# A decode step over a 1 GB KV cache: one load queue with shared 4 MB buffers, long VectorE instructions, and V streamed instead of loaded as weights

## The chip, the cores and the metric

The kernel runs on one core of one Trainium2 chip. The metric is the device time of one execution in microseconds (us). Times are medians of several runs; the profile is one more execution, taken by the hardware profiler.

In the profile PE is TensorE (matmuls), PEld its weight loads, DVE VectorE, ACT ScalarE, POOL GpSimd, SP SyncE. A core has 16 DMA engines, which carry all loads. A load "lands" when its last byte has arrived; since its parts run on all 16 engines, it has a first and a last landing, and what I call the spread is the time between the two.

## The reference

It is one token's attention over a long cache, mixed with a small feed-forward block (FFN):

```python
q = (x @ wq)                                   # x: 1x1x512, wq: 512x4096 -> 32 heads of 128
scores = einsum("bhqd,bhkd->bhqk", q, k_cache) * 128**-0.5   # k_cache: 1x32x65536x128 bf16
p = softmax(scores)
o = einsum("bhqk,bhkd->bhqd", p, v_cache)      # v_cache: 1x32x65536x128 bf16
a = o @ wo                                     # wo: 4096x512
b = (silu(x @ w_gate) * (x @ w_up)) @ w_down   # 512x1792, 512x1792, 1792x512
g = sigmoid((x * gate_w).sum())
return g * a + (1 - g) * b
```

K and V are 537 MB each. Every byte is used once, so the kernel has to stream 1087.6 MB (the profile's "HBM read") through the core. All else is small, except that each K row needs a 128-long dot product with q, which VectorE computes.

## The kernel before

A "tile" below is 16,384 rows of one head: 4 MB of K and 4 MB of V. There are 128 of them. K comes in 4 MB pieces on SyncE's queue (32 KB contiguous per partition), V in 2 MB pieces on ScalarE's queue (16 KB per partition). The dot products are computed in chunks of 32 columns (4096 rows): one multiplication into a separate buffer `prod`, four halving additions, and one reduction of the last eight.

```python
for ci, c in enumerate(seg_chunks):            # 4 chunks a tile
    m = c % DMA_MULT                           # DMA_MULT = 4
    if m == 0:
        K_big = kpool.tile([P, DMA_MULT * J, Dh], bf16)      # 2 buffers of 32 KB a partition
        nc.sync.dma_start(out=K_big, in_=A_k_cache[0, h, c*W:(c+DMA_MULT)*W, :]
                          .rearrange("(p j) d -> p j d", j=DMA_MULT * J))
    K_t = K_big[:, m * J : (m + 1) * J, :]     # J = 32
    prod = prodpool.tile([P, J, Dh], bf16)
    nc.vector.tensor_tensor(out=prod, in0=K_t, in1=q_rep, op=ALU.mult)
    half = Dh
    while half > 8:
        half //= 2
        nc.vector.tensor_tensor(out=prod[:, :, 0:half], in0=prod[:, :, 0:half],
                                in1=prod[:, :, half : 2 * half], op=ALU.add)
    nc.vector.tensor_reduce(out=S_sb[:, ci*J:(ci+1)*J], in_=prod[:, :, 0:8], axis=AXIS.X, op=ALU.add)
nc.scalar.activation(out=P_sb, in_=S_sb, func=ACT.Exp, scale=scale, accum_out=rowsum[...])
for ci, c in enumerate(seg_chunks):
    ...                                        # V_big: 2 MB on nc.scalar's queue, 3 buffers, VDMA_MULT = 2
    for j in range(J):                         # V is the weight, one column of P moves
        nc.tensor.matmul(O_ps[:, h:h+1], lhsT=V_t[:, j, :], rhs=P_sb[:, col:col+1],
                         start=(gcol == 0), stop=(gcol == NB - 1))
if h == FFN_POS:                               # FFN_POS = 0: after head 0
    _compute_ffn()
    _load_wo()
... # after all heads: totals of all heads, one normalisation, 32 projections, the mix
```

The softmax here doesn't subtract the row's maximum and nothing guards it: scores larger than these inputs give would overflow.

Of the kernel before, what the change touches and what calls it, by code (L numbers as in the profile page):

```python
# [8 lines left out]
ALU = mybir.AluOpType  # L9
AXIS = mybir.AxisListType  # L10
P = 128

KT_BUFS = 2
VT_BUFS = 3
PROD_BUFS = 2
WMAX = 4096
CHUNKS_PER_SEG = 4
LAST_HEAD_SPLIT = 1
DMA_MULT = 4
VDMA_MULT = 2  # L20
WO_ENG = "sync"
WQ_ENG = "sync"
FFN_ENG = "scalar"
FFN_POS = 0
WQ_FIRST = 0
# [3 lines left out]
def kernel(  # L29
# [24 lines left out]
    W = min(WMAX, Sk)  # L54
    assert Sk % W == 0
    NCH = Sk // W
    J = W // P
    NB = Sk // P
    CPS = min(CHUNKS_PER_SEG, NCH)
    assert NCH % CPS == 0  # L60
    SEGCOLS = CPS * J
    assert SEGCOLS <= 512
    assert NCH % DMA_MULT == 0 and NCH % VDMA_MULT == 0
    HG = 4 if H % 4 == 0 else H
    scale = float(Dh) ** -0.5

    engs = {"gpsimd": nc.gpsimd, "sync": nc.sync, "scalar": nc.scalar}

    consts = ctx.enter_context(tc.tile_pool(name="consts", bufs=1))
    psum_o = ctx.enter_context(tc.tile_pool(name="psum_o", bufs=1, space=bass.MemoryType.PSUM))  # L70
    psum_misc = ctx.enter_context(tc.tile_pool(name="psum_misc", bufs=2, space=bass.MemoryType.PSUM))
# [3 lines left out]
    xT = consts.tile([P, KT], bf16, name="xT")  # L75
    nc.sync.dma_start(out=xT, in_=A_x[0, 0, :].rearrange("(t p) -> p t", p=P))  # L76
    x_row = consts.tile([1, D], bf16, name="x_row")
    nc.sync.dma_start(out=x_row, in_=A_x[0])
    gw_row = consts.tile([1, D], bf16, name="gw_row")
    nc.sync.dma_start(out=gw_row, in_=gate_w.unsqueeze(0))  # L80
    q_bc_sb = consts.tile([P, H * Dh], bf16, name="q_bc_sb")
    b_sb = consts.tile([1, D], f32, name="b_sb")
    gval = consts.tile([1, 1], f32, name="gval")
    oT = consts.tile([P, H], bf16, name="oT")

    X_bc = consts.tile([P, KT, P], bf16, name="X_bc")
    for t in range(KT):
        nc.vector.tensor_copy(out=X_bc[:, t, :], in_=xT[:, t : t + 1].to_broadcast([P, P]))  # L88

    wq_pool_outer = None  # L90
    wq_sb = None
    awq = A_wq.rearrange("(t p) f -> p t f", p=P)
    if WQ_FIRST:
        wq_pool_outer = tc.tile_pool(name="wq_pool", bufs=1)
        wq_pool_o = wq_pool_outer.__enter__()
        wq_sb = wq_pool_o.tile([P, KT, H * Dh], bf16, name="wq_sb")
        engs[WQ_ENG].dma_start(out=wq_sb, in_=awq)

    kpool = ctx.enter_context(tc.tile_pool(name="kt", bufs=KT_BUFS))
    vpool = ctx.enter_context(tc.tile_pool(name="vt", bufs=VT_BUFS))  # L100
    prodpool = ctx.enter_context(tc.tile_pool(name="prod", bufs=PROD_BUFS))
    spool = ctx.enter_context(tc.tile_pool(name="s_sb", bufs=3))
    ppool = ctx.enter_context(tc.tile_pool(name="p_sb", bufs=3))

    def _compute_q(wq_tile):
        for g in range(H // HG):
            qg_ps = psum_misc.tile([P, HG * Dh], f32, name="qg_ps", tag="misc")
            for t in range(KT):
                nc.tensor.matmul(  # L109
                    qg_ps,  # L110
                    lhsT=X_bc[:, t, :],
                    rhs=wq_tile[:, t, g * HG * Dh : (g + 1) * HG * Dh],
                    start=(t == 0),
                    stop=(t == KT - 1),
                )
            nc.scalar.activation(  # L116
                out=q_bc_sb[:, g * HG * Dh : (g + 1) * HG * Dh], in_=qg_ps, func=ACT.Copy
            )

    if WQ_FIRST:  # L120
        _compute_q(wq_sb)
        wq_pool_outer.__exit__(None, None, None)
    else:
        with tc.tile_pool(name="wq_pool", bufs=1) as wq_pool:
            wq_sb = wq_pool.tile([P, KT, H * Dh], bf16, name="wq_sb")
            engs[WQ_ENG].dma_start(out=wq_sb, in_=awq)
            _compute_q(wq_sb)

    awg = B_w_gate.rearrange("(t p) f -> p t f", p=P)
    awu = B_w_up.rearrange("(t p) f -> p t f", p=P)  # L130
    awd = B_w_down.rearrange("(t p) n -> p t n", p=P)

    def _compute_ffn():
        with tc.tile_pool(name="ffn_w", bufs=1) as wpool:
            gu_ps = psum_misc.tile([P, 2 * FT], f32, name="gu_ps", tag="misc")
            wg_sb = wpool.tile([P, KT, F], bf16, name="wg_sb")
            engs[FFN_ENG].dma_start(out=wg_sb, in_=awg)
            wu_sb = wpool.tile([P, KT, F], bf16, name="wu_sb")
            (nc.sync if FFN_ENG == "scalar" else engs[FFN_ENG]).dma_start(
                out=wu_sb, in_=awu  # L140
            )
            wd_sb = wpool.tile([P, FT, D], bf16, name="wd_sb")
            engs[FFN_ENG].dma_start(out=wd_sb, in_=awd)
            for ft in range(FT):
                for wi, wsb in enumerate((wg_sb, wu_sb)):
                    for t in range(KT):
                        nc.tensor.matmul(  # L147
                            gu_ps[:, wi * FT + ft : wi * FT + ft + 1],
                            lhsT=wsb[:, t, ft * P : (ft + 1) * P],
                            rhs=xT[:, t : t + 1],  # L150
                            start=(t == 0),
                            stop=(t == KT - 1),
                        )
            gu_sb = consts.tile([P, 2 * FT], f32, name="gu_sb")
            nc.vector.tensor_copy(out=gu_sb, in_=gu_ps)
            eg = consts.tile([P, FT], f32, name="eg")
            nc.scalar.activation(out=eg, in_=gu_sb[:, :FT], func=ACT.Exp, scale=-1.0)
            nc.vector.tensor_scalar_add(eg, eg, 1.0)
            nc.vector.reciprocal(eg, eg)
            hprod = consts.tile([P, FT], f32, name="hprod")  # L160
            nc.vector.tensor_tensor(out=hprod, in0=gu_sb[:, :FT], in1=eg, op=ALU.mult)
            hT = consts.tile([P, FT], bf16, name="hT")
            nc.vector.tensor_tensor(out=hT, in0=hprod, in1=gu_sb[:, FT:], op=ALU.mult)
            b_ps = psum_misc.tile([1, D], f32, name="b_ps", tag="misc")
            for ft in range(FT):
                nc.tensor.matmul(  # L166
                    b_ps,
                    lhsT=hT[:, ft : ft + 1],
                    rhs=wd_sb[:, ft, :],
                    start=(ft == 0),  # L170
                    stop=(ft == FT - 1),
                )
            nc.vector.tensor_copy(out=b_sb, in_=b_ps)  # L173

            xg = consts.tile([1, D], f32, name="xg")
            s_t = consts.tile([1, 1], f32, name="s_t")
            nc.vector.tensor_tensor_reduce(
                out=xg, in0=x_row, in1=gw_row, scale=1.0, scalar=0.0,
                op0=ALU.mult, op1=ALU.add, accum_out=s_t,
            )  # L180
            eg2 = consts.tile([1, 1], f32, name="eg2")
            nc.scalar.activation(out=eg2, in_=s_t, func=ACT.Exp, scale=-1.0)  # L182
            nc.vector.tensor_scalar_add(eg2, eg2, 1.0)  # L183
            nc.vector.reciprocal(gval, eg2)

    wo_holder = {}

    def _load_wo():
        wo_pool = ctx.enter_context(tc.tile_pool(name="wo_pool", bufs=1))
        wo_sb = wo_pool.tile([P, H, D], bf16, name="wo_sb")  # L190
        engs[WO_ENG].dma_start(out=wo_sb, in_=A_wo.rearrange("(h p) n -> p h n", p=P))
        wo_holder["wo"] = wo_sb

    if FFN_POS < 0:
        _compute_ffn()
        _load_wo()

    seg_plans = []
    for h in range(H):
        if h == H - 1 and LAST_HEAD_SPLIT and CPS > 1:  # L200
            chunks = list(range(NCH))
            plan = [chunks[i : i + CPS] for i in range(0, max(NCH - CPS, 0), CPS)]
            remaining = chunks[len(plan) * CPS :]
            for cc in remaining:
                plan.append([cc])
        else:
            plan = [list(range(i, i + CPS)) for i in range(0, NCH, CPS)]
        seg_plans.append(plan)
    NSEGMAX = max(len(pl) for pl in seg_plans)

    psum_a = ctx.enter_context(tc.tile_pool(name="psum_a", bufs=1, space=bass.MemoryType.PSUM))
    psum_tot = ctx.enter_context(tc.tile_pool(name="psum_tot", bufs=1, space=bass.MemoryType.PSUM))
# [5 lines left out]
    for h in range(H):  # L218
# [60 lines left out]
        if h == FFN_POS:  # L279
            _compute_ffn()  # L280
            _load_wo()
# [65 lines left out]
```

## Time and profile before

| what | before | where it is read |
|---|---|---|
| time, median of 5 runs | 2584.27 us (2582.68 to 2587.85) | timed runs |
| span of the profiled execution | 2582.6 us | first line of the page |
| DMA engines, share taken by the two load queues | 49.7% + 49.4% | queue table |
| VectorE busy | 2470.5 us, 96% | busy table |
| TensorE busy, granted clock | 502.3 us, 19%; 0.51 | busy table; per-core list |
| last input byte to end of span | 18.4 us | DMA records and span |

These are lines of the profile page of the kernel before. First the busy table; then the span in 40 equal slices, one character or number each (busy tenths for VectorE, granted TensorE clock in tenths, busy tenths of the DMA engines, GB/s moved); then the DMA queues with packets, MB and share of the 16 engines' time; then the chain of work that ended last.

```profile
span 2582.6 us, 37723 instructions
...
PE 502.3 (19%) x16576; PEld 468.9 (18%) x16576; DVE 2470.5 (96%) x3093; ACT 58.6 (2%) x273; POOL 0.4 (0%) x5
...
DVE  4969999999999999999999999999999999999995
...
PEclk8555555555555555555555555555555555555555
DMA  9999999999999999999999999999999999999996
GB/s 404 421 399 426 427 428 431 430 429 426 428 429 428 427 430 422 429 426 428 428 427 428 427 424 431 425 428 425 429 429 422 430 426 428 425 427 430 424 427 276
DMA packets 63498, 1090.06 MB, mean 422 GB/s; under 512 B 6755, under 2 KB 12646, under 8 KB 13670
...
q1 hardware_dynamic: 24134, 547.11, 49.7%
q10 hardware_dynamic: 39200, 540.56, 49.4%
q8 instruction: 129, 2.11, 0.3%
q14 instruction: 35, 0.29, 0.0%
...
DMA 75%; DVE 18%; PE 6%; issue 0%; SPq 0%; ACT 0%; DVEq 0%; ACTq 0%
```

Both DMA and VectorE look full, and one has to decide which of the two paces. After the first four slices, which hold a dip to 399, all but the last move 422 to 431 GB/s. The queue table also shows a third kind of traffic, q8 and q14: the program's own instructions are fetched by the same engines, 2.4 MB of them for 37,723 instructions.

The next lines are groups of instructions of the kernel before, with shapes kept apart: line, engine, operation, output and input with their shapes, count, busy time, mean ns of one, and the idle time before them with what ended it.

```profile
L241 DVE TENSOR_TENSOR prod<-K_big,q_bc_sb 128x4096 bf16<-128x4096 bf16 x512 | 1147.0, 2278 | 52.4 <-DMA K_big<-in_A_k_cache_dram 51.5
L245 DVE TENSOR_TENSOR prod<-prod 128x2048 bf16<-128x2048 bf16 x512 | 600.9, 1212 | 0.0
...
L249 DVE TENSOR_REDUCE S_sb<-prod 128x32 f32<-128x256 bf16 x512 | 187.2, 403 | 0.5 <-DVE prod L245 0.5
```

Busy time over count gives 1147.0/512 = 2240 ns for a multiplication of 4096 elements per partition, less than the mean of 2278 because instructions of two chunks alternate and overlap a little. Fitting busy time over count of the five TENSOR_TENSOR sizes (4096 elements down to 256) gives 0.52 ns per element plus 107 ns per instruction; with the mean durations it is 145 ns, so about 38 ns of each instruction are hidden by the overlap.

The last views are three windows (busy time of each engine with the number of instructions, granted clock, DMA share, GB/s) and the end of the timeline (start, duration, engine, line, operation, tiles, count, idle time before and what ended it).

```profile
160.00:180.00 20.00, 1.25 (x47) 1.20 (x45) 1.34 (x1) 0.00 (x0) 0.00 (x0) 0.50 1.05 434
180.00:200.00 20.00, 1.49 (x56) 1.49 (x56) 20.00 (x25) 0.40 (x2) 0.00 (x0) 0.50 0.89 367
300.00:320.00 20.00, 3.55 (x128) 3.57 (x128) 20.00 (x26) 0.40 (x2) 0.00 (x0) 0.50 1.00 427
```

```profile
2564.67 1.87 PE L272 MATMUL O_ps<-P_sb,V_big 128*128 128x1 bf16 x64 [3.00 <-DMA V_big<-in_A_v_cache_dram]
...
2569.01 9.95 PE L301 MATMUL a_ps<-wo_sb,oT 128*1 128x512 bf16 x32 [1.51 <-DVE oT L297]
...
2578.99 0.68 DVE L310 TENSOR_TENSOR diff<-a_ps,b_sb 1x512 f32<-1x512 f32 x1 [10.04 <-PE a_ps L301]
```

The windows show where the two limits met badly. VectorE starts late (38.9 us into the span, by the timeline) and stands nearly still from 160 to 180 us, waiting for K: wo had been issued ahead of that K load, and its 1 KB rows ran from 137 to 163 us by the packet records. VectorE is then full for the next 20 us, in which DMA moves only 367 GB/s. The tail shows 32 projection matmuls taking 9.95 us after everything else.

One thing lies in the code of the kernel before and not in its profile. K is laid out with 128 consecutive rows on each partition and V with 64, so the probability in one column belongs to another row than the V row that it multiplies. I found this by reading the access patterns; no run tests it (before_v32k, below, happens to load both in one layout). These inputs hide it: the scores are near zero, the probabilities almost equal. The changed kernel uses one layout for both, so it does not have this mismatch.

### The profile page before, as it was taken

Reading aid. Unit: us, or ns where it says so; the run is one execution under the profiler, and the core shown is the slowest. Engines: PE = TensorE matmul, PEld = TensorE weight load, DVE = VectorE, ACT = ScalarE, POOL = GpSimd, SP = SyncE. Lnnn points to the kernel's source line nnn. Section 1 sums busy time; section 2 is a strip of 40 time slices with the busy share of each in tenths; the row PEclk is TensorE's granted clock in tenths of the full one; section 3 lists DMA queues with packets and bytes.
Section 4 is the critical chain, followed back from the end, with each engine's and each line's share of the span. In section 5 each row is a group of like instructions: output and inputs, shape, how many; then the busy total and the mean of one; then the engine's idle time right before and its main releaser. Section 6 shows DMA issues by size and latency. Waiting matters only on the chain.

```text
span 2582.6 us, 37723 instructions
## 1 busy us (share of the span) xinstructions
PE 502.3 (19%) x16576; PEld 468.9 (18%) x16576; DVE 2470.5 (96%) x3093; ACT 58.6 (2%) x273; POOL 0.4 (0%) x5
## 2 busy tenths in 40 slices
PE   2211112112121121112121112211121221112124
PEld 1211112111111111111111111111111111111112
DVE  4969999999999999999999999999999999999995
ACT  1000000000000000000000000000000000000000
POOL 0000000000000000000000000000000000000000
PEclk8555555555555555555555555555555555555555
DMA  9999999999999999999999999999999999999996
GB/s 404 421 399 426 427 428 431 430 429 426 428 429 428 427 430 422 429 426 428 428 427 428 427 424 431 425 428 425 429 429 422 430 426 428 425 427 430 424 427 276
DMA packets 63498, 1090.06 MB, mean 422 GB/s; under 512 B 6755, under 2 KB 12646, under 8 KB 13670
## 3 DMA queue, kind: packets, MB, share of 16 engines
q1 hardware_dynamic: 24134, 547.11, 49.7%
q10 hardware_dynamic: 39200, 540.56, 49.4%
q8 instruction: 129, 2.11, 0.3%
q14 instruction: 35, 0.29, 0.0%
HBM read 1087.64 MB, written 0.00 MB: 421 GB/s over the span
## 4 chain that ended last, share of the span: by engine, by line
DMA 75%; DVE 18%; PE 6%; issue 0%; SPq 0%; ACT 0%; DVEq 0%; ACTq 0%
DMA V_big<-in_A_v_cache_dram 72%; DVE prod L245 9%; DVE prod L241 9%; PE O_ps L272 5%; DMA K_big<-in_A_k_cache_dram 3%; DVE S_sb L249 1%; PE a_ps L301 0%; PE b_ps L166 0%; PE tot_ps L284 0%; DVE out_sb L312 0%; DVE diff L310 0%; ACT P_sb L254 0%; DVE b_sb L173 0%; SPq L76 0%; DVE tot_sb L286 0%
## 5 line engine op out<-in xcount | busy, mean ns | idle before, releaser
L241 DVE TENSOR_TENSOR prod<-K_big,q_bc_sb 128x4096 bf16<-128x4096 bf16 x512 | 1147.0, 2278 | 52.4 <-DMA K_big<-in_A_k_cache_dram 51.5
L245 DVE TENSOR_TENSOR prod<-prod 128x2048 bf16<-128x2048 bf16 (+3 forms) x2048 | 1184.3, 645 | 0.0
L272 PE MATMUL O_ps<-P_sb,V_big 128*128 128x1 bf16 x16384 | 474.7, 166 | 2025.8 <-DMA V_big<-in_A_v_cache_dram 1632.3
L272 PEld LDWEIGHTS <-V_big 128*128 128x128 bf16 x16384 | 457.4, 104 | 2043.5 <-DMA V_big<-in_A_v_cache_dram 1777.3
L249 DVE TENSOR_REDUCE S_sb<-prod 128x32 f32<-128x256 bf16 x512 | 187.2, 403 | 0.5 <-DVE prod L245 0.5
L254 ACT ACTIVATE P_sb<-S_sb 128x128 bf16<-128x128 f32 (+1 forms) x131 | 40.2, 307 | 2470.4 <-PE O_ps L272 1469.3
L254 ACT ACTIVATION_READ_ACCUMULATOR P_sb<-S_sb 128x1 f32 x131 | 24.4, 186 | 0.0
L88 DVE COPY X_bc<-xT 128x128 bf16<-128x128 bf16 x4 | 0.6, 222 | 14.5 <-DMA xT<-in_A_x_dram 14.5
L183 DVE TENSOR_SCALAR eg<-eg 1x1 f32<-1x1 f32 x1 | 0.1, 142 | 14.8 <-ACT eg L182 14.8
L109 PE MATMUL qg_ps<-wq_sb,X_bc 128*128 128x512 bf16 x32 | 8.4, 429 | 29.2 <-DMA wq_sb<-in_A_wq_dram 29.2
L286 DVE COPY tot_sb<-tot_ps 128x224 f32<-128x224 f32 x1 | 0.4, 390 | 13.4 <-PE tot_ps L284 13.4
L310 DVE TENSOR_TENSOR diff<-a_ps,b_sb 1x512 f32<-1x512 f32 x1 | 0.7, 678 | 10.0 <-PE a_ps L301 10.0
L301 PE MATMUL a_ps<-wo_sb,oT 128*1 128x512 bf16 x32 | 9.9, 486 | 1.5 <-DVE oT L297 1.5
L109 PEld LDWEIGHTS <-X_bc 128*128 128x128 bf16 x32 | 3.4, 107 | 33.7 <-DVE X_bc L88 15.9
L147 PE MATMUL gu_ps<-xT,wg_sb 128*128 128x1 bf16 x56 | 3.0, 165 | 19.3 <-DMA wg_sb<-in_B_w_gate_dram 19.3
L147 PEld LDWEIGHTS <-wg_sb 128*128 128x128 bf16 x56 | 2.6, 104 | 19.8 <-issue 19.8
L116 ACT ACTIVATE q_bc_sb<-qg_ps 128x512 bf16<-128x512 f32 x8 | 4.8, 597 | 29.8 <-PE qg_ps L109 29.8
L166 PE MATMUL b_ps<-wd_sb,hT 128*1 128x512 bf16 x14 | 5.2, 549 | 0.0
L301 PEld LDWEIGHTS <-oT 128*1 128x1 bf16 x32 | 3.1, 101 | 8.4 <-issue 4.2
L147 PE MATMUL gu_ps<-xT,wu_sb 128*128 128x1 bf16 x56 | 3.2, 166 | 0.8 <-DMA wu_sb<-in_B_w_up_dram 0.8
L147 PEld LDWEIGHTS <-wu_sb 128*128 128x128 bf16 x56 | 2.7, 104 | 0.9 <-DMA wu_sb<-in_B_w_up_dram 0.9
L173 DVE COPY b_sb<-b_ps 1x512 f32<-1x512 f32 x1 | 0.7, 678 | 1.8 <-PE b_ps L166 1.8
(24 smaller groups left out, 9.0 us busy)
## 6 DMA issues: line engine op xcount, KB each, us to landing
V_big<-in_A_v_cache_dram ACTq DMA_DIRECT2D x256, 2048.0 KB, 26.1
K_big<-in_A_k_cache_dram SPq DMA_DIRECT2D x128, 4096.0 KB, 19.8
wq_sb<-in_A_wq_dram SPq DMA_DIRECT2D x1, 4096.0 KB, 27.2
wo_sb<-in_A_wo_dram SPq DMA_DIRECT2D x1, 4096.0 KB
wu_sb<-in_B_w_up_dram SPq DMA_DIRECT2D x1, 1792.0 KB
wg_sb<-in_B_w_gate_dram ACTq DMA_DIRECT2D x1, 1792.0 KB, 19.1
wd_sb<-in_B_w_down_dram ACTq DMA_DIRECT2D x1, 1792.0 KB
xT<-in_A_x_dram SPq DMA_DIRECT2D x1, 1.0 KB, 14.9
```

Source lines behind the costliest of these rows:

```text
L109: nc.tensor.matmul(qg_ps, lhsT=X_bc[:, t, :], rhs=wq_tile[:, t, g * HG * Dh : (g + 1) * HG * Dh], start=(t == 0), stop=(t == KT - 1),)
L116: nc.scalar.activation(out=q_bc_sb[:, g * HG * Dh : (g + 1) * HG * Dh], in_=qg_ps, func=ACT.Copy)
L147: nc.tensor.matmul(gu_ps[:, wi * FT + ft : wi * FT + ft + 1], lhsT=wsb[:, t, ft * P : (ft + 1) * P], rhs=xT[:, t : t + 1], start=(t == 0), ...
L166: nc.tensor.matmul(b_ps, lhsT=hT[:, ft : ft + 1], rhs=wd_sb[:, ft, :], start=(ft == 0), stop=(ft == FT - 1),)
L173: nc.vector.tensor_copy(out=b_sb, in_=b_ps)
L241: nc.vector.tensor_tensor(out=prod, in0=K_t, in1=q_rep, op=ALU.mult)
L245: nc.vector.tensor_tensor(out=prod[:, :, 0:half], in0=prod[:, :, 0:half], in1=prod[:, :, half : 2 * half], op=ALU.add,)
L249: nc.vector.tensor_reduce(out=S_sb[:, ci * J : (ci + 1) * J], in_=prod[:, :, 0:8], axis=AXIS.X, op=ALU.add,)
L254: nc.scalar.activation(out=P_sb[:, :segcols], in_=S_sb[:, :segcols], func=ACT.Exp, scale=scale, accum_out=rowsum[:, h * NSEGMAX + sgi : h ...
L272: nc.tensor.matmul(O_ps[:, h : h + 1], lhsT=V_t[:, j, :], rhs=P_sb[:, col : col + 1], start=(gcol == 0), stop=(gcol == NB - 1),)
L301: nc.tensor.matmul(a_ps, lhsT=oT[:, h : h + 1], rhs=wo_sb[:, h, :], start=(h == 0), stop=(h == H - 1),)
L310: nc.vector.tensor_tensor(out=diff, in0=a_ps, in1=b_sb, op=ALU.subtract)
```

## The change

The intent: free memory by computing the dot products inside K's own buffer, use it for five equal buffers that K, V and all weights share, put all loads in order on one queue in 4 MB pieces, make VectorE's instructions four times as long, let TensorE stream V past four columns of P instead of loading V as weights, start on the first K piece earlier, and move all of the tail's work that can be done early ahead of the last V tile. The core of the diff, shortened:

```diff
-KT_BUFS = 2; VT_BUFS = 3; PROD_BUFS = 2; WMAX = 4096; DMA_MULT = 4; VDMA_MULT = 2
+KPP = 128; SLOTS = 5; VB = 4; DEFER = 1
+slots = ctx.enter_context(tc.tile_pool(name="slots", bufs=SLOTS))     # 32 KB a partition each
 # loads
-nc.sync.dma_start(out=K_big, ...)          # 4 MB
-nc.scalar.dma_start(out=V_big, ...)        # 2 MB
+nc.sync.dma_start(out=t[:, at:at+m, :], in_=src[:, at:at+m, :])   # K and V, m = 128: 4 MB
+load("k", 0, [KPP // 4] * 4)               # first K tile in four pieces, after 1 MB of wq
 # scores
-prod = prodpool.tile([P, J, Dh], bf16)     # J = 32
-nc.vector.tensor_tensor(out=prod, in0=K_t, in1=q_rep, op=ALU.mult)
+w = K_t[:, i*J:(i+1)*J, :]                 # parts = 1: J = 128
+nc.vector.tensor_tensor(out=w, in0=w, in1=q_rep, op=ALU.mult)
 # P times V
-for j in range(J):
-    nc.tensor.matmul(O_ps[:, h:h+1], lhsT=V_t[:, j, :], rhs=P_sb[:, col:col+1], ...)
+for i in range(KPP // VB):                 # O_ps is 4 x 512 now
+    nc.tensor.matmul(O_ps[h], lhsT=P_sb[:, i*VB:(i+1)*VB],
+                     rhs=V_t[:, i*VB:(i+1)*VB, :].rearrange("p a b -> p (a b)"), ...)
+# once per head: copy O_ps to SBUF, pick its four diagonal 128-blocks and add them (4 fp32 matmuls),
+# normalise it (deferred behind the next head's second tile)
-if h == FFN_POS: _compute_ffn(); _load_wo()
+if n == N - 2: load_tail_weights()          # wo, gate, up, down ahead of the last V tile
+load("v", N - 1, [64, 32, 16, 16])          # the last V tile in four pieces
+if n == N - 1: ffn(); 31 projections        # ahead of the last tile's P times V
```

## The prediction

> **What bounds the kernel now.** The DMA queue table shows the 16 DMA engines at 99% of their time (49.7% + 49.4% for two queues); the slices show 427 to 428 GB/s almost throughout. VectorE is busy 96%, and the windows from 300 to 500 us show both at 100%. The grouped instructions give VectorE's need per 128x16384 K tile: four chunks of 4.83 us, 19.3 us. DMA needs 8.39 MB / 428 GB/s = 19.6 us for that tile and its V. So DMA is the bound by a hair. The chain of waits agrees: 75% DMA, 18% VectorE. The last bytes land at about 2561.5 us; the remaining 21 us are PV, totals, 32 projections (10 us), output.
>
> **What changes.**
> - VectorE: the same elements in 128-column instead of 32-column instructions. By form, one costs 0.52 ns per element plus 107 ns (the reduce 1.04 ns plus 99). New tile: 8.64+4.37+2.24+1.17+0.64+1.17 = 18.2 us, 2335 us for 128 tiles, plus 32 normalisations of roughly 0.6 us: near 2360, against 2470. In-place multiplication should cost nothing (the adds already run in place). But these 110 us lie beside the DMA, off the bounding path.
> - PE: 16384 one-column matmuls with 128x128 V weights become 4096 that stream 512 V columns past 4 weight columns. In the closing projection such matmuls are 0.427 us apart for 6 us, then about 0.22. The Trainium skill, "TensorE: Matmul & The Clock Gate" (Part 1), explains this as the clock gate opening after about 3.4 us of activity[...] A tile needs 8 to 14 us of PE, below 19.6: PE rises from 19% to 40-68% without binding.
> - DMA: the same K and V bytes, all on one queue in 4 MB pieces, five shared buffers. A K buffer is freed about 21 us before its successor's turn (four 9.8 us transfers, minus 18.2), so the queue stays two transfers ahead. The skill's "DMA: Bandwidth & Descriptors" (Issuing engines are not separate DMA queues) says queues share the engines; the trace agrees: at 24-40 us one queue alone moved 427-432 GB/s. Instruction fetch (2.1 MB) falls by about 1.7 MB, worth 4 us. The early losses (slices of 421 and 399 GB/s; VectorE idle at 160-178 us while wo and FFN weights cut in) vanish: about 10 us.
> - Tail: the instruction order puts wo projections and FFN before the last two PV tiles. I estimate PE finishing about 6 us after the last byte, then merge, normalise, one projection, output: 14 us after it, against 21.
>
> **Sum.** 3 us until the first byte + 1088.3 MB / 429 GB/s (2537 us) + 14 + 2 (measured time over profiled span) = **2556 us**, 1.1% faster. Range that should hold it 8 times in 10: **2538 to 2590**. Chances: faster by over 2% 6%, within 2% 89%, slower by over 2% 5%.
>
> **What would show it.** DMA share still 99% and 427-431 GB/s in all inner slices; VectorE near 2360 us, 92%, waiting for K loads about 1.2 us per tile (150 us in all); chain above 90% DMA; 12 to 18 us between last byte and end.
>
> **What would make it wrong.** One queue leaving gaps between 4 MB transfers (at 415 GB/s: 2640 us); an in-place multiply slower than 0.52 ns per element, making VectorE the bound beyond 19.6 us per tile; PE staying at 0.427 us or above and running late at the end (up to +20 us); buffers freed too late, seen as dips in GB/s.

## The result, and the profile after

The changed kernel takes 2546.99 us (2546.63 to 2547.61, 7 runs) against 2583.48 us (13 runs) for the kernel before in the same rounds. The ratio is 0.9858, 95% interval 0.9848 to 0.9868: 1.4% faster, which is within 2%. A ratio here is the mean time of one kernel's fast runs over the mean of the other's of the same rounds, so it is not quite the ratio of the medians quoted. The prediction was 2556 us.

The same lines of the page, for the kernel after:

```profile
span 2545.3 us, 11288 instructions
...
PE 1248.9 (49%) x4610; PEld 454.5 (18%) x4610; DVE 2391.8 (94%) x897; ACT 73.9 (3%) x299; POOL 0.6 (0%) x6
...
DVE  7999999999999999999999999999999999999994
...
PEclk8777777777777776677767777777777777667777
...
GB/s 404 432 430 433 431 432 431 431 432 431 431 431 432 431 431 431 431 432 430 433 431 431 431 432 431 433 430 433 430 431 432 430 432 430 432 432 431 432 430 309
DMA packets 43497, 1088.37 MB, mean 428 GB/s; under 512 B 4403, under 2 KB 8502, under 8 KB 9782
...
q1 hardware_dynamic: 43444, 1087.66, 99.6%
q8 instruction: 36, 0.59, 0.1%
q14 instruction: 15, 0.12, 0.0%
...
DMA 67%; DVE 27%; PE 5%; issue 0%; SPq 0%; DVEq 0%; ACT 0%; ACTq 0%
```

The load queue now takes 99.6% of the DMA engines' time, and the inner slices move 430 to 433 GB/s without the dips of before. The number of packets fell from 63,498 to 43,497, since V moves in 32 KB rows, and instruction packets from 129 + 35 to 36 + 15. TensorE is busy two and a half times as long and still has half of its time free.

The groups of VectorE of the kernel after, shapes kept apart:

```profile
L150 DVE TENSOR_TENSOR slot<-slot,q_bc 128x16384 bf16<-128x16384 bf16 x127 | 1103.9, 8692 | 78.1 <-DMA slot<-in_A_k_cache_dram 72.1 <-PE O_ps L177 4.3
L154 DVE TENSOR_TENSOR slot<-slot 128x8192 bf16<-128x8192 bf16 x127 | 562.0, 4425 | 4.3
...
L158 DVE TENSOR_REDUCE S_sb<-slot 128x128 f32<-128x1024 bf16 x127 | 154.9, 1220 | 13.0
```

The elements are the same and there are 6 instructions a tile instead of 24. But each now costs about 160 ns beyond 0.52 ns per element (8692 - 16384 x 0.52 = 172, and 4425 - 8192 x 0.52 = 165; with the fitted 0.521 it is 156 to 159), and 34 ns of idle time before it (4.3 us over 127). In before the idle time was zero and instructions overlapped. The difference that I see is that each instruction now needs the result of the one before it and no second chunk alternates with it; no run tests that apart from the length of the instructions.

The same windows and the tail of the kernel after:

```profile
160.00:180.00 20.00, 9.66 (x34) 3.43 (x34) 19.02 (x7) 0.40 (x2) 0.00 (x0) 0.67 0.99 428
180.00:200.00 20.00, 10.84 (x40) 4.20 (x40) 19.16 (x7) 0.99 (x3) 0.00 (x0) 0.67 1.01 436
300.00:320.00 20.00, 10.09 (x34) 3.30 (x33) 19.13 (x7) 0.40 (x2) 0.00 (x0) 0.67 1.01 434
```

```profile
2529.72 10.31 PE L177 MATMUL O_ps<-slot,P_sb 128*4 128x512 bf16 x47
...
2540.06 0.59 ACT L204 ACTIVATE O_sb<-O_ps 4x512 f32<-4x512 f32 x1 [20.85 <-PE O_ps L177]
...
2540.70 1.05 PE L207 MATMUL c_ps<-pick,O_sb 4*128 4x1 f32 x8 [0.68 <-ACT O_sb L204]
...
2542.41 0.74 DVE L314 SCALAR_TENSOR_TENSOR out_sb<-a_ps,gval,b_sb 1x512 bf16<-1x512 f32 x1 [0.47 <-PE a_ps L283]
```

In these windows VectorE is close to 19 us busy of every 20. In the tail TensorE works through the last V pieces, then one copy, one merge and one projection are left.

**Where the 37 us came from.** From the DMA's packet records one can cut both spans at the same bytes of the input. This table holds the whole difference:

| stretch | before, us | after, us | difference |
|---|---|---|---|
| first input packet to 100 MB | 242.7 | 235.4 | 7.3 |
| 100 MB to 1000 MB | 2110.1 (426.5 GB/s) | 2087.9 (431.1 GB/s) | 22.2 |
| 1000 MB to the last byte | 209.6 | 210.4 | -0.8 |
| last byte to end of span | 18.4 | 9.9 | 8.5 |

So most of the gain is one per cent of the steady stream. The prediction explains only a small part of those 22.2 us: it put 4 us down to instruction fetch and lowered no other cost of the inner slices. The experiments look for the rest.

### The profile page after: what moved, and what is told of

Its sections match the earlier page's. It is cut to its first block, busy times and chain, and to the rows that moved or that the text cites. A ratio compares the mean times of both kernels' runs of the same rounds, so it can differ in the third digit from the quotient of the medians.

```text
span 2545.3 us, 11288 instructions
## 1 busy us (share of the span) xinstructions
PE 1248.9 (49%) x4610; PEld 454.5 (18%) x4610; DVE 2391.8 (94%) x897; ACT 73.9 (3%) x299; POOL 0.6 (0%) x6
## 2 busy tenths in 40 slices
DMA packets 43497, 1088.37 MB, mean 428 GB/s; under 512 B 4403, under 2 KB 8502, under 8 KB 9782
## 3 DMA queue, kind: packets, MB, share of 16 engines
q1 hardware_dynamic: 43444, 1087.66, 99.6%
## 4 chain that ended last, share of the span: by engine, by line
DMA 67%; DVE 27%; PE 5%; issue 0%; SPq 0%; DVEq 0%; ACT 0%; ACTq 0%
DMA slot<-in_A_k_cache_dram 54%; DVE slot L150 13%; DVE slot L154 13%; DMA slot<-in_A_v_cache_dram 12%; PE O_ps L177 4%; DVE S_sb L158 2%; DMA slot<-in_A_wq_dram 1%; SPq L100 0%; PE q_ps L126 0%; PE gu_ps L241 0%; PE b_ps L260 0%; DVE recip L199 0%; PE c_ps L207 0%; DVEq L150 0%; DVEq L158 0%
## 5 line engine op out<-in xcount | busy, mean ns | idle before, releaser
L177 PE MATMUL O_ps<-slot,P_sb 128*4 128x512 bf16 x4096 | 1170.8, 456 | 1210.8 <-DMA slot<-in_A_v_cache_dram 1210.8
L150 DVE TENSOR_TENSOR slot<-slot,q_bc 128x16384 bf16<-128x16384 bf16 (+1 forms) x131 | 1113.0, 8496 | 85.2 <-DMA slot<-in_A_k_cache_dram 79.2
L154 DVE TENSOR_TENSOR slot<-slot 128x2048 bf16<-128x2048 bf16 (+3 forms) x524 | 1106.0, 2112 | 17.4
L177 PEld LDWEIGHTS <-P_sb 128*4 128x4 bf16 x4096 | 398.8, 97 | 1957.0 <-issue 1571.1
L158 DVE TENSOR_REDUCE S_sb<-slot 128x128 f32<-128x1024 bf16 (+1 forms) x131 | 156.5, 1195 | 13.0
L163 ACT ACTIVATE P_sb<-S_sb 128x128 bf16<-128x128 f32 x128 | 39.6, 309 | 2425.8 <-DVE S_sb L158 2368.5
L207 PE MATMUL c_ps<-pick,O_sb 4*128 4x1 f32 x256 | 33.5, 248 | 35.1 <-ACT O_sb L204 35.1
L207 PEld LDWEIGHTS c_ps<-pick,O_sb 4*128 4x128 f32 x256 | 30.8, 186 | 51.2 <-ACT O_sb L204 50.0
L163 ACT ACTIVATION_READ_ACCUMULATOR P_sb<-S_sb 128x1 f32 x128 | 23.9, 186 | 0.0
L189 PE MATMUL tot_ps<-rowsum,ones 128*128 128x4 f32 x64 | 12.5, 266 | 19.9 <-ACT P_sb L163 19.6
L126 PE MATMUL q_ps<-slot,X_bc 128*128 128x512 bf16 x32 | 11.1, 521 | 19.6 <-DMA slot<-in_A_wq_dram 19.6
L204 ACT ACTIVATE O_sb<-O_ps 4x512 f32<-4x512 f32 x32 | 18.4, 575 | 23.3 <-PE O_ps L177 23.2
## 6 DMA issues: line engine op xcount, KB each, us to landing
slot<-in_B_w_up_dram SPq DMA_DIRECT2D x1, 1792.0 KB, 14.2
```

Source lines behind the costliest of these rows:

```text
L126: nc.tensor.matmul(q_ps, lhsT=X_bc[:, t, :], rhs=wq_sb[:, t, g * QG : (g + 1) * QG], start=(t == 0), stop=(t == KT - 1),)
L150: nc.vector.tensor_tensor(out=w, in0=w, in1=q_rep, op=ALU.mult)
L154: nc.vector.tensor_tensor(out=w[:, :, 0:half], in0=w[:, :, 0:half], in1=w[:, :, half : 2 * half], op=ALU.add,)
L158: red = nc.vector.tensor_reduce(out=S_sb[:, i * J : (i + 1) * J], in_=w[:, :, 0:8], axis=AXIS.X, op=ALU.add)
L177: nc.tensor.matmul(O_ps[h], lhsT=P_sb[:, i * VB : (i + 1) * VB], rhs=V_t[:, i * VB : (i + 1) * VB, :].rearrange("p a b -> p (a b)"), start ...
L189: nc.tensor.matmul(tot_ps, lhsT=ones, rhs=rowsum[:, h * CH : (h + 1) * CH], start=True, stop=True)
```

## The experiments

The question is what made the steady stream faster. My first theory was that the bytes per row of a DMA matter (**rows**): V's 16 KB rows cost more than 32 KB rows. The rivals were that the instruction fetch takes DMA time (**fetch**), that VectorE was the real limit of before (**VectorE**), and that one queue serves better than two (**queue**). Each kernel is the changed one with one part undone, unless said otherwise. All outputs were correct. The changed kernel itself was not run again, so differences from its 2546.99 us compare medians across chips; the kernel before had medians of 2583.2 to 2584.0 us, and 2587.8 us where its runs fell into two groups near 2583.5 and 2588. I therefore do not read differences of 1 to 2 us.

### two_queues: V back on ScalarE's queue

```diff
-nc.sync.dma_start(out=t[:, at : at + m, :], in_=src[:, at : at + m, :])
+q = nc.sync if which == "k" else nc.scalar
+q.dma_start(out=t[:, at : at + m, :], in_=src[:, at : at + m, :])
```

> The kernel after, with the V loads issued on ScalarE's queue again and K on SyncE's, still 4 MB each. The stretch from 100 to 1000 MB moved at 426.5 GB/s before and 431.1 GB/s after; this asks whether the one queue did that. Queue theory: back to 426.5 to 428 GB/s, 2565 to 2575 us. Rival theories (length of V rows, VectorE's longer instructions, fewer instructions to fetch): 431 GB/s and 2545 to 2550 us. If V issues get stuck behind ScalarE's other work, the DMA share itself should dip below 99%, which would be a third thing and not the queue count.

Measured: 2578.02 us (2573.24 to 2590.03), ratio 0.9981 (0.9963 to 0.9998). The loss is 31 us, but not because two queues share worse: slices in which both have work move 431 to 432 GB/s, as with one. The loss sits in a few dips. These are the GB/s line of its page's slices, one of its windows, and its first issues of loads after 60 us in its timeline (start, duration, queue; the row with x2 joins two issues, one at its start and one at its end):

```profile
GB/s 406 375 423 431 431 426 432 432 416 424 423 431 430 432 432 432 432 431 431 429 427 425 432 432 431 429 430 432 431 431 431 431 428 431 420 430 424 430 416 268
```

```profile
80.00:100.00 20.00, 10.60 (x36) 3.55 (x37) 20.00 (x10) 0.81 (x4) 0.00 (x0) 0.65 0.66 260
```

```profile
88.04 10.66 SPq L101 DMA_DIRECT2D slot<-in_A_k_cache_dram  x2
...
88.04 0.31 ACT L164 ACTIVATE P_sb<-S_sb 128x128 bf16<-128x128 f32 x1 [44.23 <-DVE S_sb L159]
...
98.36 0.37 ACTq L101 DMA_DIRECT2D slot<-in_A_v_cache_dram  x1
```

What follows: no load is issued from 60 to 88.04 us, then one K load, and the next K and the next V load only at 98.36 us; the exponential on ScalarE had waited 44 us for scores. In the window from 80 us the DMA engines were 66% busy. My reading is that five buffers shared by two queues are no longer filled in the order in which they are needed, since each queue issues when its own engine gets there, and ScalarE also has the exponentials to do. That reading is argued from these times and not tested apart. What is shown is that two queues as such cost no bandwidth and that the loss lies where issuing has gaps. This agrees with the Trainium skill, "DMA: Bandwidth & Descriptors" (Issuing engines are not separate DMA queues), which says that DMAs from different engines run on the same 16 DMA engines and that issuing from several saves only issue time. It cost more than it saved.

### v_2mb: V in 2 MB pieces with 16 KB rows, one queue

```diff
-load("v", n, whole if n < N - 1 else [64, 32, 16, 16])
+load("v", n, [KPP // 2] * 2 if n < N - 1 else [64, 32, 16, 16])
```

> The kernel after, one queue, with each V tile loaded as two pieces of 2 MB, so 16 KB per partition row as before. Row-length theory: 426.5 to 428 GB/s, 2565 to 2575 us. Queue theory and VectorE theory: 431 GB/s, 2545 to 2550 us[...].

Measured: 2555.42 us, ratio 0.9886 (0.9873 to 0.9899): 8.4 us slower than the changed kernel, and between what the two theories expected. The steady stream falls from 431.1 to 429.4 GB/s. By the trace's packet records, a 16 KB packet takes 615.0 ns and a 32 KB packet 1217.8 ns, so two small ones cost 12 ns more than one large.

### rows16k and rows8k: all of K and V in shorter rows

The size of each transfer stays 4 MB; only the contiguous run on each partition shrinks to 16 KB (RUN = 64) or 8 KB (RUN = 32).

```diff
-src = cache[...].rearrange("(p j) d -> p j d", j=KPP)
+src = cache[...].rearrange("(b p j) d -> p b j d", p=P, j=RUN)
```

> The kernel after with both K and V laid out as two runs of 16 KB per partition instead of one of 32 KB; still one DMA of 4 MB per tile, one queue. In the records of after one 32 KB packet takes 1217.7 ns, in v_2mb one of 16 KB 615.0 ns, so a packet costs about 12 ns on top of its bytes. If that cost is per packet (row length): each 32 KB takes 1230 ns, 1.0% more, about 426.7 GB/s from 100 to 1000 MB and 2570 to 2574 us. If the slower V of v_2mb was a cost per DMA issued (twice as many there): no change, 2546 to 2549 us.

> The same with four runs of 8 KB. Per-packet theory, extrapolated with 12.3 ns per packet: 313.6 ns for 8 KB, 3.0% more than with 32 KB, 418 GB/s, 2615 to 2630 us. Per-DMA theory: 2546 to 2549 us.

Measured: 2566.30 us with 16 KB rows (ratio 0.9932, 0.9919 to 0.9944) and 2604.47 us with 8 KB rows (ratio 1.008, 1.0064 to 1.0095). Both are a little below what the rows theory expected, so my cost per packet was too high, but its form holds. The packets take 615.4 and 314.4 ns. Against 1217.7 ns for 32 KB that is 2 x 615.4 - 1217.7 = 13.1 ns for one extra packet, and 4 x 314.4 - 1217.7 = 39.9 ns for three. In wall time it is 19.3 us over 2048 extra packets per engine and 57.5 us over 6144, 9.4 ns each both times; the records of packets that follow each other on an engine overlap by 3 to 4 ns, which is about the difference. With rows of 32, 16 and 8 KB each tile's period in the steady state is 19.50, 19.65 and 19.95 us, and VectorE starts a tile 0.1 us or less after its K landed (median) in all three.

What follows: the row length sets the stream's speed even at 8 to 32 KB, with a fixed cost per packet, and it costs about the same per packet in 2 MB transfers (v_2mb: 8.4 us over 1024 extra packets per engine, 8.2 ns) as in 4 MB ones. The Trainium skill, "DMA: Bandwidth & Descriptors" (Why small descriptors are slow), names a fixed overhead of about three cycles per packet and calls merging packets worth it only at 256 B or less. Here a cost per packet, whether it is that one or not, still makes 0.76% of the time at 16 KB and 2.3% at 8 KB.

### score4: VectorE's instructions short again

```diff
-score(n, 4 if n == 0 else 1)
+score(n, 4)
```

> The kernel after, with VectorE's instructions cut back to 32 columns for all tiles (four parts each, as before). VectorE theory: the old rate was the rate at which VectorE freed K buffers, so with 19.3 us per tile the time goes back up to 2565 to 2585 us. Queue and row theories: VectorE at 19.3 us still hides behind 19.45 us of DMA per tile: 2546 to 2552 us, VectorE busy about 2470 us (97%) or, if the dependent steps cost more than they did in the kernel before, up to 2550 us and then the time follows VectorE.

Measured: 2564.69 us, ratio 0.9922 (0.9909 to 0.9935). That is just under what the VectorE theory expected, and 17.7 us slower than the changed kernel, the largest loss of the single parts. Yet the trace does not look like a VectorE limit. These are its busy table, its second queue of instruction fetches (15 packets in the changed kernel), its wait for K, and one window near the end:

```profile
PE 1252.7 (49%) x4610; PEld 458.6 (18%) x4610; DVE 2485.6 (97%) x3183; ACT 72.9 (3%) x299; POOL 0.6 (0%) x6
...
q14 instruction: 34, 0.28, 0.0%
```

```profile
DVE slot L150 <- DMA slot<-in_A_k_cache_dram: 16.9, 30, 5.1
```

```profile
2500.00:2510.00 10.00, 9.52 (x32) 3.14 (x31) 9.87 (x13) 0.40 (x2) 0.00 (x0) 0.74 0.38 117
```

VectorE still waits for K 30 times, and the tile period is 19.63 us where its work is 19.4 us (2485.6/128); by the landing records a tile's scores begin 0.12 us after its K landed. The steady stream fell to 429.9 GB/s. And the last 88 MB took 221.6 us instead of 210.4. In that window the DMA engines are only 38% busy: most of them have finished and a few are behind. The records show this growing: the time between the first and the sixteenth engine's landing of one 4 MB load rises from 2.5 us early to 17.3 us; in the changed kernel it rises from 2.6 to 10.8 us. The bytes queued ahead at issue shrink from 9.9 to 3.9 MB as that happens (10.2 to 8.2 MB in the changed kernel).

The landing records settle what happens there. Take the time from the last landing of one 4 MB load to the last landing of the next. In both kernels it is 9.71 us, except for single steps of 0.97 us on top. Between 100 and 2440 us the changed kernel has 8 such steps, about 280 us apart, and score4 has 25, about 93 us apart; in sum the last landing falls behind by 7.8 us in the one and 23.9 us in the other, and the difference of 16.1 us is nearly the whole 17.7. Each step comes within 15 us after an instruction fetch on q14, and the number of steps goes with VectorE's instructions (897 and 3183). The packet records show the price: such a fetch of 8 KB takes 0.33 us, and the data packet right behind it takes 1.88 us instead of 1.22. There are as many such pairs as steps, 8 and 25. Each of them delays the engine that lands last, so these fetches fall on one engine, and every load waits for it.

What follows: VectorE's form costs 17.7 us, but through the fetches of its instructions, which delay one DMA engine. Three runs below test this.

### score4_rows16k: both at once

If the time were the larger of two limits, adding short rows to score4 should cost much less than it did alone. If both costs fall on the DMA engines they add: 2546.99 + 17.7 + 19.3 = 2584.0 us.

```diff
-score(n, 4 if n == 0 else 1)
+score(n, 4)
-src = cache[...].rearrange("(p j) d -> p j d", j=KPP)
+src = cache[...].rearrange("(b p j) d -> p b j d", p=P, j=RUN)      # RUN = 64
```

> Both undone at once in the kernel after: 32-column VectorE instructions and 16 KB rows. Alone they cost 17.7 us (score4) and 19.3 us (rows16k). If the time is the larger of two nearly tied limits, VectorE's and the DMA's, they overlap: 2566 to 2572 us, 1 to 5 us over the larger one. If the costs are independent and add: 2582 to 2585 us.

Measured: 2584.33 us, ratio 1.0001 (0.9988 to 1.0013). They add to within 0.3 us. The time is not the larger of a VectorE limit and a DMA limit; both changes slow the same stream. Its last landings come 9.79 us apart, as in rows16k, with score4's 25 steps on top.

### dve_busy: VectorE longer, without more instructions to speak of

One small addition per tile into a scratch buffer lengthens VectorE's work.

```diff
+if parts == 1:
+    nc.vector.tensor_tensor(out=scr, in0=w[:, 0:3, :], in1=w[:, 3:6, :], op=ALU.add)
```

> The counterpart: the kernel after plus one VectorE instruction of 384 columns per tile (about 0.35 us, no use made of it), so that VectorE is as loaded as in score4 but with 127 more instructions instead of 2286. Fetch theory: 2547 to 2549 us, spread as in after (11 us). VectorE theory: score4's time, 2560 to 2566 us.

Measured: 2548.38 us, ratio 0.9851 (0.9835 to 0.9867). This is its busy table:

```profile
PE 1248.7 (49%) x4610; PEld 455.2 (18%) x4610; DVE 2434.7 (96%) x1024; ACT 73.1 (3%) x299; POOL 0.6 (0%) x6
```

VectorE was busy 2434.7 us instead of 2391.8, and the time rose by 1.4 us, too little to be read as a cost. VectorE's time is off the bounding path, as predicted: of 43 us, nothing of that order shows. The added work was less than half of score4's 94 us, though the text on record calls it equal, so this run alone does not exclude a limit of VectorE at score4's load; the steps in score4's landings do, since between them its loads come as fast as in the changed kernel. Here there are 9 steps for 1024 instructions of VectorE, 8.6 us in sum.

### act_nops: more instructions, on an engine that has nothing to do

Eighteen tiny copies per tile on ScalarE, which was 3% busy: 2268 more instructions in the program, 11,288 to 13,556, nearly score4's 13,729.

```diff
+for i in range(NOPS):                       # NOPS = 18
+    nc.scalar.activation(out=junk[:, i:i+1], in_=P_sb[0:1, i:i+1], func=ACT.Copy)
```

> The kernel after plus 18 one-element instructions per tile on ScalarE, which is 97% idle: 2268 more instructions, about as many as score4 added on VectorE (2286), and no work on any engine that matters. In score4 VectorE started each tile 0.1 us after its K had landed, so VectorE did not set the pace; its landings came every 19.63 us instead of 19.50, the 16 DMA engines drifted apart faster (17 us between the first and the last engine's share of one DMA, against 11), and 40 fetch packets of 8 KB ran on the instruction queue instead of 21. Fetch theory: the fetches delay one of the 16 engines, on which every tile waits: 2558 to 2566 us, about 40 such packets, spread up to 17 us. VectorE theory: 2546 to 2549 us.

Measured: 2554.06 us, ratio 0.9873 (0.9858 to 0.9888): 7.1 us slower than the changed kernel and 5.7 us slower than dve_busy, which ran on the same chip. The queue table of its page has the fetches:

```profile
PE 1254.6 (49%) x4610; PEld 460.8 (18%) x4610; DVE 2391.7 (94%) x897; ACT 297.5 (12%) x2567; POOL 0.6 (0%) x6
...
q14 instruction: 33, 0.27, 0.0%
```

It has 18 more packets on q14 than the changed kernel, of 8 KB each, and VectorE is unchanged at 2391.7 us. The landings of one load spread to 14.2 us instead of 10.8.

What follows: instructions cost DMA time even where the engine that runs them is idle, so the fetch theory has a real effect. It was smaller than expected (11 to 19 us), and the landing records show why. Up to 950 us nearly all of its steps come after VectorE's fetches, as before; from 1370 us there is instead a step of 0.68 us about every 120 us, each after a fetch of another kind: 0.31 us, and the data packet behind takes 1.59 us instead of 1.22. Only their number rose when ScalarE got more instructions (6 to 22 between 100 and 2440 us; VectorE's went from 8 to 9), so they are ScalarE's. They delay another engine than VectorE's do, and cost little until that engine has become the last. Score4's fetches fall on the engine that is the last already, so each of them counts, and with 0.97 us instead of 0.68. The records do not name the engines; that they are two is concluded from the steps.

### v_weights: V as the weight again, 16384 one-column matmuls

```diff
-for i in range(KPP // VB):
-    nc.tensor.matmul(O_ps[h], lhsT=P_sb[:, i*VB:(i+1)*VB], rhs=V_t[:, i*VB:(i+1)*VB, :]..., ...)
+for i in range(KPP):
+    nc.tensor.matmul(O_ps[h], lhsT=V_t[:, i, :], rhs=P_sb[:, i:i+1], ...)
```

> The kernel after, with only the PE part undone: V is again the 128x128 weight operand of 16384 one-column matmuls, P the moving column, no merge at the end of a head. Stream: 1.5 MB more instruction fetch, 3 to 4 us longer. Tail: a tile takes 3.7 us of PE instead of 9.7, so PE ends about 1.5 us after the last byte instead of 6.7, and 2 us of copy and merge go: 7 us shorter. Sum 2543 to 2546 us. If the streaming form of the matmul is itself what lets the DMA run faster, 2560 us or more instead.

Measured: 2557.79 us, ratio 0.9895 (0.9882 to 0.9907). I had expected 2543 to 2546 us, since the shorter tail should have gained more than the fetch cost. This is its queue of instruction fetches:

```profile
q8 instruction: 130, 2.13, 0.3%
```

Its last input byte lands at 2551.5 us against 2535.4, 16.1 us later, while the tail after it shrinks from 9.9 to 4.8 us. Of the 16 us, 7.8 lie between 100 and 1000 MB (429.5 GB/s) and 7.7 after it, where the engines' landings spread to 23.6 us. It has 35,321 instructions instead of 11,288, and 94 more fetch packets of 16 KB at 1.07 us each; spread evenly over 16 engines they would take 6.3 us (94 x 1.068 / 16). The data packet behind each takes 1.71 us instead of 1.22, which makes it 9 us (an estimate: 94 x 1.56 / 16). Up to 2440 us the last landings have 43 steps after fetches, 22.5 us in sum, 14.7 more than in the changed kernel: the engine that is the last gets more than its even share. TensorE, at 20% busy and clock 0.51, cannot be the limit.

What follows: the instructions removed by the new matmul form were worth 16 us of the stream, not 4, and the form itself cost 5 us in the tail.

### slots4: four shared buffers

```diff
-SLOTS = 5
+SLOTS = 4
```

> The kernel after with four shared buffers instead of five. By the order of the transfers a K buffer is then free about one transfer (10 us) before its successor's turn instead of two. If one transfer of lead is enough: 2546 to 2550 us and the DMA share unchanged. If the queue needs more lead than that, dips in GB/s and 2560 us or more; the fifth buffer would then be a part of the gain.

Measured: 2546.04 us, ratio 0.9853 (0.9837 to 0.9868): the same as with five. The bytes queued ahead fall to between 6.0 and 4.3 MB and the landings spread to only about 8 us. The fifth buffer buys nothing here, and a lead as short as 4.3 MB (score4's was 3.9 late) costs nothing by itself.

### before_v32k: the kernel before with 32 KB rows for V

The rows theory must also hold in the kernel before. V comes in 4 MB pieces with two buffers; to fit, one FFN weight takes over another's buffer, so it is loaded later.

```diff
-VT_BUFS = 3; VDMA_MULT = 2
+VT_BUFS = 2; VDMA_MULT = 4
-wd_sb = wpool.tile([P, FT, D], bf16, name="wd_sb");  engs[FFN_ENG].dma_start(out=wd_sb, in_=awd)
+wd_sb = wpool.tile([P, FT, D], bf16, name="wd_sb", tag="wgd")     # loaded after gate and up are used
```

> The kernel before with one part of the change alone: V loaded in 4 MB pieces with 32 KB rows (two buffers instead of three of half the size; to make it fit, one FFN weight waits for another's buffer, once, in the first head). Row-length theory: 128 tiles x 8 rows per DMA engine x (2 x 615.9 - 1217.7 = 14 ns) = 14 us less: 2567 to 2573 us, V packets at 1218 ns. Rival: VectorE at 19.3 us per tile set the pace of before, then no gain, 2580 us or more. A third outcome would be over 2584 us because two V buffers are too few.

Measured: 2589.31 us, ratio 1.002 (1.0008 to 1.0033): slower, the third outcome named. Its reason there, that two V buffers are too few, was not tested. The rows theory was right about the stream, whose last byte lands at 2554.8 us instead of 2564.2, 9 us earlier. But the span ends 32.8 us after it instead of 18.4. One window of it, at the start:

```profile
100.00:120.00 20.00, 3.55 (x128) 3.57 (x128) 14.57 (x19) 0.40 (x2) 0.00 (x0) 0.50 0.99 425
```

VectorE is idle for 5 of these 20 us, waiting for K (at 160 to 180 us it has 5.6 us of work). In this run it also starts at 43.6 us, 4.7 us later than in before, and it has no room to make that up: its last scores end 15 us after the last byte, where those of before end 10 us ahead of it. What follows: the kernel before has two limits so close together that relieving one hands the time to the other. Its VectorE starts at 38.9 us where the changed kernel's starts at 11.1 us, and needs 19.3 us of a 19.6 us tile. That the early start and the uninterrupted feed were needed to make use of the faster stream is my reading; no run adds them alone.

### last_head_w: the best version

v_weights showed a tail 5 us shorter for V as the weight, since it needs no copy and no merge. This kernel keeps the new form for 31 heads and uses the old one for the last head only.

```diff
 def pv(n):
+    if h == H - 1:
+        for i in range(KPP):
+            nc.tensor.matmul(O_ps[h], lhsT=V_t[:, i, :], rhs=P_sb[:, i:i+1], ...)
+        return
 def finish(h):
+    if h == H - 1:
+        outs[h] = O_ps.pop(h)
+        return
```

> A candidate to beat both: the kernel after, but in the last head alone V is the weight operand (as in v_weights), so that PE is not late behind the last bytes and no copy and merge follow. In v_weights the end came 6.0 us after the last byte, in after 11.1 us. 768 more PE instructions cost under 1 us of fetch. Expected 2541 to 2543 us. If PE's lag at the end does not matter, 2547 us.

Measured: 2542.26 us (2541.70 to 2543.34), ratio 0.9839 (0.9826 to 0.9852). The end of its timeline:

```profile
2534.86 0.58 PE L181 MATMUL o_col<-P_sb,slot 128*128 128x1 bf16 x16 [0.20 <-DMA slot<-in_A_v_cache_dram]
...
2536.13 0.58 PE L181 MATMUL o_col<-P_sb,slot 128*128 128x1 bf16 x16 [0.68 <-DMA slot<-in_A_v_cache_dram]
2536.75 0.16 DVE L213 TENSOR_TENSOR oT<-o_col,recip 128x1 bf16<-128x1 f32 x1 [9.43 <-PE o_col L181]
...
2537.59 0.74 DVE L330 SCALAR_TENSOR_TENSOR out_sb<-a_ps,gval,b_sb 1x512 bf16<-1x512 f32 x1 [0.68 <-PE a_ps L299]
```

TensorE follows the last pieces as they land: it waits for each instead of working off a backlog. The tail is 4.8 us instead of 9.9 (the text on record read them as 6.0 and 11.1; the difference is the same), and the stream is unchanged (last byte at 2535.6 us against 2535.4). It beats both kernels; its range does not touch that of the changed kernel.

## Why the prediction was right, and where it was not

The time (2546.99 us) fell in the range around 2556 us and the class, within 2%, was the one given 89%. The range was wide: it held even the time of the kernel before. Of the 36.5 us gained, the forecast had 28 (2584.27 - 2556). Term by term:

1. **"DMA is the bound by a hair."** Right. After the change the load queue takes 99.6% of the engines' time, dve_busy's 43 us of VectorE work cost 1.4 us, and VectorE starts each tile 0.1 us or less after its K landed. More exactly it is the last of the 16 DMA engines that bounds.
2. **"1088.3 MB / 429 GB/s (2537 us)."** First to last byte took 2533.7 us, which is 429 GB/s on average, as forecast. That is partly luck: the steady stream ran at 431.1 GB/s, faster than the forecast gave a reason for, while the first 100 MB ran at 425 and the last 88 MB at 417. Of the 9 us by which 2556 was too high, 3.3 lie here, 4.1 in the tail, and the rest in the first microseconds and the rounding. What the prediction missed is that the same bytes are not the same time: v_2mb puts V's longer rows at 8.4 us.
3. **"Instruction fetch falls by about 1.7 MB, worth 4 us."** The bytes were right (2.4 to 0.7 MB by the queue table). The worth was too small: v_weights loses 16 us of stream with 1.5 MB more of it. An average over 16 engines, at the rate of data, is the wrong price: a fetch also lengthens the data packet behind it, and each load waits for the last of the 16.
4. **VectorE "near 2360, against 2470 ... these 110 us lie beside the DMA".** Measured 2391.8. I took the 107 ns per instruction from a kernel where two chunks alternate; in one dependent series it is 160 ns. That the time lies beside the DMA is right. But the 24 to 6 instructions per tile did matter, through their fetches: score4 loses 17.7 us.
5. **PE "from 19% to 40-68% without binding".** Right, 49%. A tile takes 8 to 10 us; its first 6 to 14 matmuls come about 0.427 us apart and then 0.216, so the clock opened after 2.5 to 6 us of activity, and in the closing projection of before after 5.9 us. The Trainium skill, "TensorE: Matmul & The Clock Gate" (Part 1), describes such a gate with a window of about 3.4 us, and warns that the count varies; the trace agrees in kind, with a count that varies from tile to tile.
6. **"The early losses ... vanish: about 10 us."** Measured 7.3 us to 100 MB. Of the weights it names, only wo cut in at that time.
7. **Tail "14 us after it, against 21".** Measured 9.9 against 18.4, below the "12 to 18 us" given as a sign. PE finished 4.6 us after the last byte (I said about 6), and what follows took 5.2 us (I said 8).
8. **"Chain above 90% DMA", "waiting for K loads ... 150 us".** Wrong as signs: the chain is 67% DMA and 27% VectorE, and the wait is 79 us. When a load waits for its buffer, the chain runs back through the scores that freed that buffer, and so counts VectorE where VectorE does not pace. dve_busy and the landings decide this, not the chain.

Together, the single reversals come close to the 22.2 us of the steady stream: between 100 and 1000 MB they cost 8.2 us (v_2mb, rows), 7.8 us (v_weights, fetch) and 5.8 us (score4, fetch), 21.7 us in sum. That they add was tested for one pair alone (score4_rows16k), and no run undoes all three; in the kernel before, the longer V rows alone gave 7.5 us of this stretch (before_v32k). Over whole times they sum to 8.4 + 10.8 + 17.7 = 36.9 us, close to the 36.5 us of the change; that is partly chance, since the change also gained 7 us early and 8.5 us in the tail, and since score4 and v_weights lose time at the end to the engines' spread, which the kernel before does less (the landings of its V loads settle at a spread of 9.6 us, those of K at 4).

What is not settled: why the data packet behind a fetch takes longer, and by different amounts for the three engines, and why VectorE's fetches all fall on one DMA engine.

## What to carry to other kernels

When a kernel streams at over 99% of its DMA time, everything that passes through the DMA engines is on the path: the number of rows and the number of instructions too, priced at the slowest of the engines and not at their average. Decide between two limits that both look full by adding a little work to one of them, as dve_busy did, and look whether time is lost evenly or in steps, and after what; a busy share and a chain of waits did not tell. And where two limits lie within 2%, relieving only one gives nothing (before_v32k), while a cheaper form for the bulk may be the wrong one for the last piece (last_head_w).

## What the Trainium skill lacked or had wrong

- "DMA: Bandwidth & Descriptors" (Why small descriptors are slow) treats the fixed cost per packet as a matter of 256 B and less. Here 13 ns per extra packet in the records, 9.4 ns in wall time, cost 19.3 us of 2547 with 16 KB rows and 57.5 us with 8 KB rows.
- "Runtime: NRT & Kernel Launch" (Instruction fetch mechanics) says that an engine's instructions are refilled in 16 KiB blocks and that crossing a block boundary is mostly hidden. In a DMA-bound kernel it is not: 2268 more instructions on an idle engine cost 6 to 7 us, and 24,033 more in v_weights, TensorE's, cost 16 us of the stream. A fetch packet of 16 KB took 1.07 us on a DMA engine, and VectorE's and ScalarE's came in packets of 8 KB, 0.31 to 0.33 us.
- No page that I found says that the 16 DMA engines drift apart in a long stream, or that instruction fetches do it. The first and last landing of one 4 MB load were 2.6 us apart early and 10.8 us late in the changed kernel, up to 23.6 us in v_weights, and each tile waits for the last. Between 100 and 2440 us of the changed kernel the last landing fell behind in 8 steps of 0.97 us, each after one 8 KB fetch for VectorE, and otherwise by no more than 0.1 us at a time.
- "VectorE: DVE Perf Modes" (Rules for kernel authors) advises fewer operations, which held (VectorE busy 2391.8 us, against 2485.6 in score4). It gives no figure for two alternating series: 107 ns each beyond the elements here, against 160 ns and 34 ns of idle time for the longer instructions in one dependent series.
- "DMA: Bandwidth & Descriptors" (Where 436 GB/s comes from) says that for loads from HBM the limit near 358 GB/s binds; its own single-core measurement reaches 425. This lone core held 431.1 GB/s over 900 MB, close to the page's 435. (Elsewhere the page ties the lower figure to both cores of a pair streaming, which no run here tests.)
